# End of the attention stage: filler products, last sums in two PSUM banks, one copy on another engine, transposes last

## The chip, the cores and the metric

One core of a Trainium2 chip runs the whole kernel. The metric is the time of one execution on the device in microseconds (us). PE is TensorE, DVE is VectorE, ACT is ScalarE, POOL is GpSimd, SP is SyncE, whose queue issues the DMAs. Where the text writes L625, it means line 625 of the kernel before.

## What is computed

Attention with rotary positions over 4 batches of 8 heads, 576 positions, head width 64, all in float32; then a soft mixture of 8 experts with 4 slots each; then a two-layer network. The part that matters here is the middle one. `logits` are the products of the 2304 tokens x (width 512) with `phi` for 32 slots; a softmax over the tokens gives the weights with which the tokens are summed into slot inputs; these go through the first and second layer of their expert.

```python
logits = x @ phi
d = logits - logits.max(0, keepdims=True)
d = np.exp(d)
d /= d.sum(0, keepdims=True) + 1e-09
slot_input = d.T @ x
...
    h = np.maximum(slot_input[e] @ w1[e], 0.0)
    slot_out[e] = h @ w2[e]
```

A softmax over the slots of each token, from the same logits, later combines the outputs of the slots.

## The kernel before, in words

The heads are worked in 16 pairs, four pairs to a batch of 576 tokens. The first three batches of tokens have their logits, exponentials and sums made while the attention of later pairs runs (`batch`). The last batch cannot hide behind attention, so it is split in two halves of its tokens, `half(0)` with 256 and `half(1)` with 320 of them, that overlap with each other. Everything here is issued in an order written out by hand: each engine runs its own instructions strictly in the order in which the program lists them, and semaphores make an engine wait for what another one writes. The program lists the steps of the two halves as calls `h0[k]()` and `h1[k]()` (L945 to L970), where k counts the functions that `half` returns:

- 0 `logits` (L546): products of the tokens with phi, on PE. 1 `logits2`.
- 2 `soft` (L568): the maximum over the tokens (L569) and a few steps on one column, on DVE.
- 3 `expo` (L577): the exponential with its sum on ACT (L578), and scale factors; a scaling of the sums so far on DVE (L581) or the scaled small identity `ss` (L585).
- 4 `keep` (L587): ACT copies the logits to SBUF, for the later combine step.
- 5 `d_t` (L590): PE transposes the exponentials, 32 slots x 128 tokens at a time, into PSUM, and DVE copies them to `d` in SBUF (L600).
- 6 `s_mm` (L602): the sums, products of `d` with the tokens; L609 and, for the 64 tokens left over in half 1, L614. In half 1 the sums of the first two column blocks are in rows 0 to 63 and those of the last two in rows 64 to 127 of one PSUM bank.
- 8 `merge` (L616): DVE scales half 0's sums and adds them to the sums so far, `s_b[0]`.
- 7 `slots` (L619): ACT copies the two parts of half 1's sums to SBUF in two steps (L623); PE transposes and adds the merged sums (four products with `ss`, L625) and half 1's sums (four products, L629) in one PSUM tile; DVE copies the result to `si` (L630). What is passed as `between` is issued between the two groups of products.
- 9 `total` (L632): the sum of the weights, on DVE.

After half 1's `d_t`, five PE transposes of the kept logits (`lt3`, L964) go as `between` into `slots`, and ACT copies them to `lt` (L968, L969). Then the first layer begins (`layer1`, L990): 64 f32 products with 32 weight columns and 512 moving columns. It needs `si` and the weights `w`, whose loads SP issues (`load_w`, L129), the later ones when earlier tiles release their places in SBUF. A product of f32 operands runs as two instructions on PE, an f32 transpose as one. PSUM tiles come from pools of fixed banks: `ps_m` and `ps_u` have one bank each, `ps_mx` one pair of banks, `ps_st` two pairs.

Of the kernel before, what the change touches and what calls it, by code (L numbers as in the profile page):

```python
# [7 lines left out]
F32 = mybir.dt.float32  # L8
# [3 lines left out]
ACTF = mybir.ActivationFunctionType  # L12
# [9 lines left out]
NSLOT = 32  # L22
# [43 lines left out]
def attn_softmoe_mlp_kernel(ctx: ExitStack, tc: tile.TileContext, qk, v, cst, phi, w1, w2, w_in, w_out, out):  # L66
    nc = tc.nc
    pe, act, dve, pool, sp = nc.tensor, nc.scalar, nc.vector, nc.gpsimd, nc.sync
# [13 lines left out]
    cst_sb = const.tile([128, 256], F32, tag="cst", name="cst_sb")  # L82
    ident = cst_sb[:, 0:128]
# [106 lines left out]
    with tc.manual_schedule():  # L190
        with ExitStack() as t1:
            def mkpool(name, bufs, space=None):
                return t1.enter_context(tc.tile_pool(name=name, bufs=bufs, **({"space": space} if space else {"side": left})))
# [8 lines left out]
            ps_mx = mkpool("ps_mx", 1, PSUM)  # L202
            ps_u = mkpool("ps_u", 1, PSUM)
            ps_m = mkpool("ps_m", 1, PSUM)
# [177 lines left out]
            et, er, u_ps, xt, xq = {}, {}, {}, {}, {}  # L382
# [63 lines left out]
            def x_c(p, c):  # L446
                return xq[p][:, 2 * c:2 * c + 2].rearrange("p h d -> p (h d)")
# [90 lines left out]
            hb = []  # L538

            def half(h):  # L540
                i, o, w_ = 3 + 2 * h, QO[h], QN[h]
                xs = [xt[12 + j] for j in range(4)]
                d = p_r.tile([128, 3, NSLOT], F32, tag=f"dh{h}", name=f"dh{h}")
                ps = {}
# [44 lines left out]

                def d_t():  # L590
                    if h:
                        t = ps_mx.tile([128, 2, 512], F32, tag="mx", name=f"dps{i}")[:, 0]
                    else:
                        t = ps_u.tile([128, 512], F32, tag="u", name=f"dps{i}")
                    for c in range(2):
                        pe.transpose(t[:, NSLOT * c:NSLOT * c + NSLOT], ps["dt"][0:32, 128 * c:128 * c + 128], ident[0:32, 0:32])
                    for r in HEAD[0:2 * h]:
                        pe.matmul(t[r, 2 * NSLOT:3 * NSLOT], lhsT=ps["dt"][0:32, 256:320], rhs=ident[0:32, 0:32], start=True, stop=True, skip_group_check=True)
                    n = 2 + h
                    dve.tensor_copy(out=d[:, 0:n], in_=t[:, 0:NSLOT * n].rearrange("p (c s) -> p c s", c=n))  # L600

                def s_mm():  # L602
                    t = ps["s"] = (ps_m if h else ps_u).tile([128, DM], F32, tag="m" if h else "u", name=f"sps{i}")
                    js = (0, 2, 1, 3) if h else range(4)
                    for j in js:
                        w = slice(128 * j, 128 * j + 128)
                        g = 64 * h * (j // 2)
                        for c in range(2):
                            pe.matmul(t[g + 32 * c:g + 32 * c + 32, w], lhsT=d[:, c], rhs=x_c(12 + j, 2 * h + c), start=j % (2 if h else 4) == 0, stop=h == 0, skip_group_check=True)  # L609
                    for j in js:  # L610
                        for hd, r in enumerate(HEAD[0:2 * h]):
                            o = 128 * j + 64 * hd
                            g = 64 * (j // 2) + 32 * hd
                            pe.matmul(t[g:g + 32, o:o + 64], lhsT=d[r, 2], rhs=xq[12 + j][r, 8], start=False, stop=True, skip_group_check=True)  # L614

                def merge():  # L616
                    dve.scalar_tensor_tensor(out=s_b[0][0:64], in0=ps["s"][0:64], scalar=sc[0:64, 3:4], in1=s_b[0][0:64], op0=ALU.mult, op1=ALU.add)
# [1 line left out]
                def slots(between):  # L619
                    o = hb[1][:, 0:DM]  # L620
                    t = ps_st.tile([128, 2, 512], F32, tag="st", name="slots")[:, :, 0:2 * NSLOT].rearrange("p b (k s) -> p b k s", k=2)
                    for r, c in ((slice(0, 64), slice(0, 256)), (slice(64, 128), slice(256, 512))):
                        act.activation(out=o[r, c], in_=ps["s"][r, c], func=ACTF.Copy)  # L623
                    for k in range(4):
                        pe.matmul(t[:, k // 2, k % 2], lhsT=s_b[0][:, 128 * k:128 * k + 128], rhs=ps["ss"], start=k % 2 == 0, stop=False, skip_group_check=True)  # L625
                    between()
                    for k in range(4):
                        r = HEAD[k // 2]
                        pe.matmul(t[:, k // 2, k % 2], lhsT=o[r, 128 * k:128 * k + 128], rhs=stack_i[r, 0:NSLOT], start=False, stop=True, skip_group_check=True)  # L629
                    dve.tensor_copy(out=si.rearrange("p (b k) s -> p b k s", b=2), in_=t)  # L630

                def total():  # L632
# [4 lines left out]
                    dve.reciprocal(out=den, in_=den)  # L637

                return logits, logits2, soft, expo, keep, d_t, s_mm, slots, merge, total

            CHUNKS = [[(128 * c, min(128, S - 128 * c)) for c in range(5)]] * 4
# [227 lines left out]
            a, b = rot[0], rot[1] = rotary(0), rotary(1)  # L869
# [65 lines left out]
            t = ps_mx.tile([128, 2, 512], F32, tag="mx", name="u_31")  # L935
# [9 lines left out]
            h0, h1 = hb[0], hb[3]  # L945
# [3 lines left out]
            assert not tasks, tasks  # L949
            h0[3]()  # L950
            h1[0]((3,))
            h0[5]()
            h1[2]()
            h0[4]()
            h1[3]()
            h0[6]()
            h1[5]()
            h0[8]()
            h1[4]()
            t = ps_mx.tile([128, 2, 512], F32, tag="mx", name="lt3_ps")  # L960

            def lt3():
                for i, (o, n) in enumerate(CHUNKS[3]):
                    pe.transpose(t[0:n, 0, NSLOT * i:NSLOT * i + NSLOT], hb[2][0:32, o:o + n], ident[0:32, 0:32])  # L964

            h1[6]()
            h1[7](lt3)
            act.activation(out=lt[:, 15:19], in_=t[:, 0, 0:4 * NSLOT].rearrange("p (c s) -> p c s", c=4), func=ACTF.Copy)  # L968
            act.activation(out=lt[0:64, 19], in_=t[0:64, 0, 4 * NSLOT:5 * NSLOT], func=ACTF.Copy)  # L969
            h1[9]()  # L970

        def pool2(name, bufs, space=None, st=ctx, **kw):
# [300 lines left out]
    t = ps_o.tile([128, 512], F32, tag="o", name="g0_ps")[:, 0:128]  # L1273
# [28 lines left out]
    for n, (j, k) in enumerate(seq):  # L1302
        ghi, glo = gt.pop((j, k))
        for i in range(NI):
            if (j, k, i) not in ((0, 0, 0), (0, 0, 1), (0, 0, 2)):
                products(j, k, i, ghi, glo)
            t = ops[j, i]
# [7 lines left out]
            if k == 15:  # L1315
                o = g2.tile([128, DM], F32, tag="os", bufs=6, name=f"os{j}_{i}")
# [52 lines left out]
```

## Time and profile before

| | |
|---|---|
| median of 3 runs | 563.58 us (562.36 to 564.84) |
| profiled execution, whole | 562.48 us |
| span of its instructions | 560.7 us |
| PE busy in the span | 542.5 us, 97% |
| DVE, ACT, POOL busy | 312.7, 298.8, 112.5 us |
| mean granted clock of PE | 0.993 of full speed |

The profile is of one execution, and the sums that are made from its rows stand against its own 562.48 us. The span runs from the first instruction to the last; 1.8 us of the whole lie around it. Times in the rows are us from the start of the span. A matmul's end is modelled, and its products overlap, so the time from the start of one group to the start of the next tells more than their busy time.

### The profile page before, as it was taken

The numbers are of one execution on the slowest core, as the hardware profiler recorded it, in microseconds if no ns is written. First come the engines' busy times: TensorE is split into PE (matmuls) and PEld (weight loads), VectorE is DVE, ScalarE is ACT, GpSimd is POOL, SyncE is SP. The second block draws the span as 40 slices with busy tenths as digits, with TensorE's granted clock in tenths as the row PEclk, the third lists the DMA queues.
The fourth block names the chain that finished last, engine by engine and source line by source line (L and its number), as shares of the span: only waits on it lengthen the run. The fifth ranks groups of instructions, "written<-read, shape, count | busy, mean of one in ns | idle before, by whom it ended". The sixth has DMA issues, their size and how long they took to land.

```text
span 560.7 us, 15277 instructions
## 1 busy us (share of the span) xinstructions
PE 542.5 (97%) x6283; PEld 437.4 (78%) x6283; DVE 312.7 (56%) x826; ACT 298.8 (53%) x582; POOL 112.5 (20%) x105
## 2 busy tenths in 40 slices
PE   8989999999999999999999989999999999999996
PEld 5668888888888988888862347788888888888885
DVE  4667666676665567654130448877454444644442
ACT  3656666666676566664420346775443444533342
POOL 3475433312333323200000031412000000000000
PEclk9999999999999999999998999999999999999999
DMA  8325777645664675663799885461030000300002
GB/s 330 117 88 196 237 235 264 211 159 173 225 219 147 211 275 180 224 213 92 297 344 365 290 351 191 131 198 63 2 112 1 1 0 0 114 1 1 0 1 112
DMA packets 38720, 89.31 MB, mean 159 GB/s; under 512 B 10598, under 2 KB 13948, under 8 KB 36732
## 3 DMA queue, kind: packets, MB, share of 16 engines
q1 hardware_dynamic: 38652, 88.36, 45.3%
q8 instruction: 49, 0.80, 0.6%
q14 instruction: 19, 0.16, 0.1%
HBM read 78.20 MB, written 7.60 MB: 153 GB/s over the span
## 4 chain that ended last, share of the span: by engine, by line
PE 81%; ACT 7%; DVE 5%; issue 3%; DMA 2%; SPq 1%; ACTq 0%; DVEq 0%
PE ops L1266 11%; PE ops L1268 11%; PE ops L1267 11%; PE u L431 10%; PE st L398 7%; PE psmx L327 3%; PE l L996 3%; PE hps L1173 3%; ACT e L402 3%; PE st_r L411 3%; PE l L1017 3%; PE xps L459 2%; ACT relu L335 2%; PE u L425 2%; PE psmx L343 2%
## 5 line engine op out<-in xcount | busy, mean ns | idle before, releaser
L1180 DVE TENSOR_TENSOR hps<-hps,g 128x384 f32<-128x384 f32 x96 | 50.5, 562 | 81.5 <-ACT g L1177 81.4
L1177 ACT ACTIVATE g<-hps 128x384 f32<-128x384 f32 x96 | 43.2, 489 | 85.0 <-PE hps L1173 84.7
L348 DVE CUSTOM_DVE_ANT_0 relu<-psmx,relu 128x288 f32<-128x288 f32 x142 | 59.4, 454 | 44.7 <-ACT e L402 38.3
L402 ACT ACTIVATE e<-st 128x512 f32<-128x512 f32 (+1 forms) x128 | 76.4, 650 | 10.4 <-PE st L398 10.4
L431 PE MATMUL u<-v,e 128*64 128x65 f32 x2048 | 80.1, 224 | 0.3 <-ACT e L402 0.3
L1266 PE MATMUL ops<-wo_hi,ghi 128*128 128x512 f32 x198 | 77.8, 393 | 0.7 <-ACT ghi L1183 0.7
L1267 PE MATMUL ops<-wo_lo,ghi 128*128 128x512 f32 x198 | 77.4, 391 | 0.3 <-POOL wo_lo L1161 0.3
L1268 PE MATMUL ops<-wo_hi,glo 128*128 128x512 f32 x198 | 77.6, 392 | 0.0
L431 PEld LDWEIGHTS u<-v,e 128*64 128x64 f32 x2048 | 70.9, 137 | 6.7 <-issue 2.6
L335 ACT ACTIVATE relu<-psmx 128x576 f32<-128x576 f32 x63 | 40.9, 651 | 52.5 <-PE psmx L327 40.6
L277 POOL TENSOR_TENSOR raw<-raw,tab 128x576 f32<-128x576 f32 x28 | 40.3, 1439 | 114.4 <-DMA raw<-in_qk_dram 68.3
L1186 DVE TENSOR_TENSOR glo<-hps,ghi 128x384 fp32r<-128x384 f32 x96 | 50.0, 552 | 4.0
L1183 ACT ACTIVATE ghi<-hps 128x384 fp32r<-128x384 f32 x96 | 46.2, 491 | 10.4 <-DVE hps L1180 10.3
L1268 PEld LDWEIGHTS ops<-wo_hi,glo 128*128 128x128 f32 x198 | 37.2, 188 | 8.1 <-DVE glo L1186 0.3
L1266 PEld LDWEIGHTS ops<-wo_hi,ghi 128*128 128x128 f32 x198 | 37.2, 188 | 7.9 <-ACT ghi L1183 0.9
L1267 PEld LDWEIGHTS ops<-wo_lo,ghi 128*128 128x128 f32 x198 | 37.2, 188 | 7.1 <-POOL wo_lo L1161 0.8
L274 POOL TENSOR_TENSOR raw<-raw,tab 128x576 f32<-128x576 f32 x28 | 41.3, 1475 | 0.0
L398 PE MATMUL st<-hi 64*128 64x256 f32 (+1 forms) x256 | 39.3, 301 | 0.0
L398 PE MATMUL st<-hi,lo 64*128 64x256 f32 (+1 forms) x256 | 38.2, 292 | 0.0
L398 PE MATMUL st<-mq,neg_a 64*128 64x256 f32 (+1 forms) x256 | 38.2, 292 | 0.0
L398 PE MATMUL st<-lo,hi 64*128 64x256 f32 (+1 forms) x256 | 38.2, 292 | 0.0
L1266 PE MATMUL ops<-wo_hl,ghi 128*128 128x512 f32 x90 | 35.2, 391 | 0.0
(228 smaller groups left out, 993.5 us busy)
## 6 DMA issues: line engine op xcount, KB each, us to landing
w<-in_w_dram SPq DMA_DIRECT2D x64, 512.0 KB
raw<-in_qk_dram SPq DMA_DIRECT2D x14, 1152.0 KB
w_out_raw<-in_w_out_dram SPq DMA_DIRECT2D x16, 512.0 KB
w_in_raw<-in_w_in_dram SPq DMA_DIRECT2D x12, 512.0 KB
v<-in_v_dram SPq DMA_DIRECT2D x16, 325.0 KB
out_dram<-os SPq DMA_DIRECT2D x18, 256.0 KB
w_in<-w_in SPq DMA_DIRECT2D x8, 256.0 KB
w_in_raw<-in_w_in_dram SPq DMA_DIRECT2D x2, 1024.0 KB
```

The lines of the kernel that those rows point to most:

```text
L335: act.activation(out=r, in_=pair[:, :, 0:HS], func=ACTF.Relu)
L348: dve.tensor_tensor_reduce(out=r[:, hd], in0=t[hd], in1=r[:, hd], scale=1.0, scalar=-3.0e38, op0=ALU.add, op1=ALU.max, accum_out=mxs[p % 2 ...
L398: pe.matmul(st[:, hd, 0:n], lhsT=a, rhs=b, start=i == 0, stop=i == 3, skip_group_check=True)
L402: act.activation(out=e[:, :, 0:n], in_=st[:, :, 0:n], func=ACTF.Exp, scale=0.125)
L431: pe.matmul(u[q:q + 64, 2 * i + hd], lhsT=e[:, hd, o:o + 64], rhs=x[:, hd], start=n == 0 and i + hd == 0, stop=n == 4, skip_group_check=True)
L1177: act.activation(out=g[i], in_=t[i], func=ACTF.Sigmoid)
L1180: dve.tensor_tensor(out=t[i], in0=t[i], in1=g[i], op=ALU.mult)
L1183: act.activation(out=ghi[:, i], in_=t[i], func=ACTF.Copy)
L1186: dve.tensor_tensor(out=glo[:, i], in0=t[i], in1=ghi[:, i].bitcast(F32), op=ALU.subtract)
L1266: pe.matmul(t, lhsT=a, rhs=wo_hi[k], start=k == 0, stop=False)
L1267: pe.matmul(t, lhsT=a, rhs=wo_lo[k], start=False, stop=False)
L1268: pe.matmul(t, lhsT=b, rhs=wo_hi[k], start=False, stop=k == 15)
```

## The change

`half(0)`'s copy of its transposed exponentials moves from DVE to ACT, and its `keep` is listed ahead of it. Half 1's sums go to two PSUM banks, one for rows 0 to 63 and one for rows 64 to 127, and their two copies to SBUF are made by ACT and by DVE. Products of the identity with 64 constant columns, whose results nobody reads, are listed on PE at five places: 3 after half 0's transposes, 3 after its sums, 4 after half 1's transposes, 3 inside `slots` in the place of the logit transposes, 4 after these, which now come behind `slots`. Nothing else is added, and no DMA is touched.

```diff
--- before.py
+++ after.py
@@ -589,7 +589,8 @@
 
                 def d_t():
                     if h:
-                        t = ps_mx.tile([128, 2, 512], F32, tag="mx", name=f"dps{i}")[:, 0]
+                        ps["two"] = ps_mx.tile([128, 2, 512], F32, tag="mx", name=f"dps{i}")
+                        t = ps["two"][:, 0]
                     else:
                         t = ps_u.tile([128, 512], F32, tag="u", name=f"dps{i}")
                     for c in range(2):
@@ -597,21 +598,27 @@
                     for r in HEAD[0:2 * h]:
                         pe.matmul(t[r, 2 * NSLOT:3 * NSLOT], lhsT=ps["dt"][0:32, 256:320], rhs=ident[0:32, 0:32], start=True, stop=True, skip_group_check=True)
                     n = 2 + h
-                    dve.tensor_copy(out=d[:, 0:n], in_=t[:, 0:NSLOT * n].rearrange("p (c s) -> p c s", c=n))
+                    o, i_ = d[:, 0:n], t[:, 0:NSLOT * n].rearrange("p (c s) -> p c s", c=n)
+                    if h:
+                        dve.tensor_copy(out=o, in_=i_)
+                    else:
+                        act.activation(out=o, in_=i_, func=ACTF.Copy)
 
                 def s_mm():
                     t = ps["s"] = (ps_m if h else ps_u).tile([128, DM], F32, tag="m" if h else "u", name=f"sps{i}")
+                    ts = ps["ss2"] = (t, ps["two"][:, 1] if h else t)
                     js = (0, 2, 1, 3) if h else range(4)
                     for j in js:
                         w = slice(128 * j, 128 * j + 128)
                         g = 64 * h * (j // 2)
+                        t = ts[j // 2]
                         for c in range(2):
                             pe.matmul(t[g + 32 * c:g + 32 * c + 32, w], lhsT=d[:, c], rhs=x_c(12 + j, 2 * h + c), start=j % (2 if h else 4) == 0, stop=h == 0, skip_group_check=True)
                     for j in js:
                         for hd, r in enumerate(HEAD[0:2 * h]):
                             o = 128 * j + 64 * hd
                             g = 64 * (j // 2) + 32 * hd
-                            pe.matmul(t[g:g + 32, o:o + 64], lhsT=d[r, 2], rhs=xq[12 + j][r, 8], start=False, stop=True, skip_group_check=True)
+                            pe.matmul(ts[j // 2][g:g + 32, o:o + 64], lhsT=d[r, 2], rhs=xq[12 + j][r, 8], start=False, stop=True, skip_group_check=True)
 
                 def merge():
                     dve.scalar_tensor_tensor(out=s_b[0][0:64], in0=ps["s"][0:64], scalar=sc[0:64, 3:4], in1=s_b[0][0:64], op0=ALU.mult, op1=ALU.add)
@@ -619,8 +626,9 @@
                 def slots(between):
                     o = hb[1][:, 0:DM]
                     t = ps_st.tile([128, 2, 512], F32, tag="st", name="slots")[:, :, 0:2 * NSLOT].rearrange("p b (k s) -> p b k s", k=2)
-                    for r, c in ((slice(0, 64), slice(0, 256)), (slice(64, 128), slice(256, 512))):
-                        act.activation(out=o[r, c], in_=ps["s"][r, c], func=ACTF.Copy)
+                    a, b_ = ps["ss2"]
+                    act.activation(out=o[0:64, 0:256], in_=a[0:64, 0:256], func=ACTF.Copy)
+                    dve.tensor_copy(out=o[64:128, 256:512], in_=b_[64:128, 256:512])
                     for k in range(4):
                         pe.matmul(t[:, k // 2, k % 2], lhsT=s_b[0][:, 128 * k:128 * k + 128], rhs=ps["ss"], start=k % 2 == 0, stop=False, skip_group_check=True)
                     between()
@@ -949,24 +957,32 @@
             assert not tasks, tasks
             h0[3]()
             h1[0]((3,))
+            h0[4]()
             h0[5]()
             h1[2]()
-            h0[4]()
+            busy = ps_m.tile([128, 512], F32, tag="m", name="busy0")
+
+            def fill_up(n, t):
+                for _ in range(n):
+                    pe.matmul(t[:, 0:64], lhsT=ident, rhs=cst_sb[:, 0:64], start=True, stop=True, skip_group_check=True)
+
             h1[3]()
+            fill_up(3, busy)
             h0[6]()
+            fill_up(3, busy)
             h1[5]()
             h0[8]()
             h1[4]()
+            fill_up(4, busy)
+            h1[6]()
+            busy = ps_u.tile([128, 512], F32, tag="u", name="busy1")
+            h1[7](lambda: fill_up(3, busy))
             t = ps_mx.tile([128, 2, 512], F32, tag="mx", name="lt3_ps")
-
-            def lt3():
-                for i, (o, n) in enumerate(CHUNKS[3]):
-                    pe.transpose(t[0:n, 0, NSLOT * i:NSLOT * i + NSLOT], hb[2][0:32, o:o + n], ident[0:32, 0:32])
-
-            h1[6]()
-            h1[7](lt3)
+            for i, (o, n) in enumerate(CHUNKS[3]):
+                pe.transpose(t[0:n, 0, NSLOT * i:NSLOT * i + NSLOT], hb[2][0:32, o:o + n], ident[0:32, 0:32])
             act.activation(out=lt[:, 15:19], in_=t[:, 0, 0:4 * NSLOT].rearrange("p (c s) -> p c s", c=4), func=ACTF.Copy)
             act.activation(out=lt[0:64, 19], in_=t[0:64, 0, 4 * NSLOT:5 * NSLOT], func=ACTF.Copy)
+            fill_up(4, busy)
             h1[9]()
 
         def pool2(name, bufs, space=None, st=ctx, **kw):
```

## Rows read from the trace of the kernel before

**Rows 1.** The page: span, busy time and instructions of each engine, PE's clock in 40 slices.

```profile
span 560.7 us, 15277 instructions
...
PE 542.5 (97%) x6283; PEld 437.4 (78%) x6283; DVE 312.7 (56%) x826; ACT 298.8 (53%) x582; POOL 112.5 (20%) x105
...
PEclk9999999999999999999998999999999999999999
```

**Rows 2.** Busy time by stretch: us, each engine's busy us, granted clock, DMA share, GB/s.

```profile
288.00:290.00 2.00, 1.61 (x22) 1.19 (x22) 0.89 (x4) 1.12 (x4) 0.00 (x0) 1.00 0.96 332
290.00:292.00 2.00, 1.66 (x39) 1.37 (x39) 0.91 (x2) 0.50 (x2) 0.00 (x0) 1.00 1.04 394
292.00:294.00 2.00, 1.61 (x21) 1.40 (x24) 0.36 (x3) 0.61 (x3) 0.00 (x0) 0.73 1.02 390
294.00:296.00 2.00, 2.00 (x12) 0.54 (x16) 0.69 (x4) 0.00 (x0) 0.00 (x0) 0.50 1.04 384
298.00:300.00 2.00, 2.00 (x16) 0.51 (x12) 0.00 (x0) 0.00 (x0) 0.00 (x0) 0.56 0.91 305
330.00:332.00 2.00, 1.66 (x19) 1.29 (x22) 1.82 (x5) 2.00 (x5) 1.20 (x1) 1.00 1.04 418
332.00:334.00 2.00, 1.28 (x34) 0.93 (x26) 0.33 (x2) 0.56 (x2) 2.00 (x3) 1.00 1.04 432
```

**Rows 3.** The chain of waits in order of time: start us, us, engine and line.

```profile
287.81 0.23 DVE dh L600
288.04 0.41 DVE mb L569
...
293.60 0.30 DVE si L630
```

**Rows 4.** The timeline, 284 to 300: start us, us, engine, line, instructions, idle before and releaser.

```profile
285.01 0.66 PE L459 MATMUL xps<-cst_sb,x 128*64 128x128 f32 x8
...
285.50 0.28 PE L461 MATMUL xps<-cst_sb,x 128*64 128x64 f32 x4
...
285.71 1.82 PE L559 MATMUL lgh<-xt,phi_sb 128*32 128x320 f32 x24
...
286.94 0.49 DVE L581 TENSOR_SCALAR s_b<-s_b,sc 128x512 f32<-128x512 f32 x1 [1.43 <-ACT sc L580]
...
287.46 0.31 PE L596 MATMUL dps<-cst_sb,last_logits 32*128 32x32 f32 x2
...
288.09 1.07 PE L609 MATMUL sps<-x,dh 128*32 128x128 f32 x16 [0.32 <-DVE dh L600]
...
289.45 0.30 PE L596 MATMUL dps<-cst_sb,last_logits 32*128 32x32 f32 x2 [0.29 <-ACT last_logits L578]
...
290.21 0.73 DVE L617 SCALAR_TENSOR_TENSOR s_b<-sps,sc,s_b 64x512 f32<-64x512 f32 x1
...
290.35 0.65 PE L609 MATMUL sps<-x,dh 128*32 128x128 f32 x16 [0.36 <-DVE dh L600]
...
291.28 1.08 PE L625 MATMUL slots<-ss,s_b 128*128 128x32 f32 x8
291.47 0.78 ACT L623 ACTIVATE last_logits<-sps 64x256 f32<-64x256 f32 x2 [1.57 <-PE sps L614]
...
292.29 0.46 PE L964 MATMUL lt_ps<-cst_sb,last_logits 32*128 32x32 f32 x5
...
292.68 0.88 PE L629 MATMUL slots<-cst_sb,last_logits 64*128 64x32 f32 x8
292.78 0.28 ACT L968 ACTIVATE lt<-lt_ps 128x128 f32<-128x128 f32 x1 [0.53 <-PE lt_ps L964]
...
293.95 6.50 PE L996 MATMUL l<-w,si 128*32 128x512 f32 x32 [0.39 <-DVE si L630]
```

**Rows 5.** The timeline, 328 to 336: the first group of transposes.

```profile
329.40 0.86 PE L1079 MATMUL cst<-cst_sb,ch 128*128 128x128 f32 x5
```

**Rows 6.** Waits of SP's DMA queue, 250 to 360: us in all, times, longest.

```profile
SPq L129 <- PE l L996: 15.5, 4, 8.2
```

## The prediction

> **What bounds the kernel now.** I read the page first: TensorE (PE) is busy for 542.5 of the 560.7 us, and its clock row has one dent, a single digit, just behind the middle of the span [rows 1]. The busy times by stretch give the dent its size [rows 2]: the granted clock is 1.00 up to 292, 0.73 in 292:294, 0.50 in 294:296, 0.56 in 298:300, and full again later. [...] So the clock is low from 292.92 to 299.76. What the engine did before the fall stands in the rows before it: 288 to 294 have 1.6 us of 2 busy each, with waits in between and small products. Being busy by these rows does not hold the clock by itself: 332:334 shows less, 1.28 us of 2, and the clock stays at 1.00.
>
> What runs at half speed is mostly the first layer: it starts at 293.95 [rows 4] and fills its stretches [rows 2]. 299.76 - 293.95 = 5.81 us at half clock is 2.90 us of work, so 2.90 us is what a full clock gives back here.
>
> The chain of waits shows what stands in front of it [rows 3]: the copy of the first half's weights on VectorE (DVE), the maximum of the second half on the same engine behind that copy, then, after ACT's (ScalarE's) exponential and the products, the last copy. The timeline has PE's own order [rows 4]. From start to start: transposes 287.46, first sums 288.09, transposes 289.45, last sums 290.35, slot products (L625) 291.28, five logit transposes 292.29, second slot products (L629) 292.68, first layer 293.95.
>
> **The change part by part, in the order of time.** The price of a filler: it is a product of 128 weight columns with 64 moving columns in f32, which runs as two instructions. The nearest row is L625, 128x128 weights with 32 columns: its eight instructions start at 291.28 and the next group starts at 292.29, 1.01 us with the hand-over, 0.126 each [rows 4]. So four fillers cost 1.01 us, three 0.76, all seventeen 34 x 0.126 = 4.28 us. That width doubles costs nothing extra if the weight load sets the pace, as the same row suggests. Lower end: x products with half as many weight columns, eight from 285.01 to 285.50, 0.061 each [rows 4]; I take the nearer row. Upper end: a single instruction's 0.135 (1.08 / 8).
>
> *Copy to ACT, keep first.* DVE loses the copy of 0.23 us; the maximum, which started at 288.04 behind it on the chain [rows 3], can start when the logits end, 285.71 + 1.82 = 287.53 (DVE's scaling is done at 287.43 [rows 4]). With the start-up of a DVE step I take 287.65, so the maximum and the exponential come 0.39 us earlier, and the second transposes could start at 289.45 - 0.39 = 289.06. On ACT the copy is priced by a 128x128 copy, 0.28 us [rows 4], against 0.23, so the weights are no more than 0.05 us later; below nothing there is no reason for. It fits on ACT between keep and the exponential at 288.4. Keep already came before in time, so its move costs nothing.
>
> *Three fillers before the first sums.* Two transposes take 0.16 (five took 0.39), to 287.62; fillers to 288.38. The first sums start there in place of 288.09: +0.29.
>
> *Three fillers after them.* The sixteen instructions need about 0.91 us (I take 1.07 less 0.16 for the last one's tail), to 289.29; fillers to 290.05. The second transposes were at 289.45 and could have come at 289.06: what DVE gained is covered by fillers, and PE stands +0.60.
>
> *Four fillers after the second transposes.* These take about 0.38 to issue (an estimate: 0.16 as above, and four narrower products in 0.22), 290.43; fillers to 291.44, where the last sums start: before, 290.35, +1.09. Their weights are ready at 290.05 + 0.90 = 290.95 (0.90 is 289.45 to 290.35), so 0.49 of this is over the wait. The merge on DVE (0.73 us [rows 4]) also comes later, by 0.6, and ends near 291.6, still ahead of the slot products at 292.37.
>
> *Two banks, two engines.* ACT's two half copies took 0.78 us in series [rows 4]; now one half each runs on ACT and DVE at once, about 0.4 us. The copies end near 292.9; PE is in the slot products until 293.38 and then in fillers, so this is worth nothing here. Without fillers it would be covered too.
>
> *Transposes last, fillers in their place.* Three fillers replace five transposes: 0.76 against 0.39, +0.37; L629 starts at 294.14 against 292.68, +1.46. L629 took 0.88 us, part of it at the low clock; I take 0.5 to issue at full clock (ends: 0.4 and 0.88). Then transposes 0.39 and four fillers 1.01: the first layer can start at 296.04 on PE. The si copy is ready long before: L629 ends by 295.0, copy 0.30 [rows 3], 295.4 with hand-overs. ACT's two logit copies move behind too; nobody waits for them before the combine step, behind the first layer. Start +2.09.
>
> *Loads.* No DMA is added. The weight loads at this point wait for PE's first layer to release slots [rows 6], so they follow it in both directions.
>
> *Sum.* +2.09 for the later start, -2.90 for the full clock: -0.81 us. The profiled execution took 562.48; 561.7. That execution is 1.1 us below the median 563.58, and the runs shown spread from 562.36 to 564.84, so against the median this is -0.33%.
>
> [...] From 329.40 on PE transposes in groups of four and five, with copies between (the first such group: [rows 5]), and 330:332 and 332:334 have a clock of 1.00 [rows 2]: no transpose there pulled it down. [...]
>
> **The rivals.**
>
> *The clock falls all the same* (0.27), the one on the slower side. Place: between the last sums and the first layer. The fillers resemble L625, wide weight loads and few columns, and L625 is just what ran when the clock fell, with PE busy. The fillers' columns are twice as many, and they replace real waits, which speaks against it. Price: a low stretch as long as the one seen, 6.84 us, now filled without waits, costs 3.42 us: 561.7 + 3.4 = 565.1, 2.6 us above the profiled execution. It decides as soon as a low stretch lasts longer than 1.6 us within the first layer, since 0.81 us is all that the forecast gains. A low stretch half as long again would cost 1.7 us more (566.8).
>
> *The fillers fit into the waits* (0.15). At the lower end, 0.061 per instruction, three take 0.37 and four 0.49; following the same steps the first sums start at 288.09, the second transposes at 289.37, the last sums at 290.27, L629 at 292.58, the first layer at 293.96, no later than before. Then the full 2.90 us stays: 559.6. For it: PE's waits in 288 to 294 are 1.1 us of 6 by busy time, more by start times. Against: L625 itself, whose load width is the fillers' own. [...] The row shows 126 ns with hand-over and decides.
>
> *A later stage takes the gain back* (0.08): the first layer ends 0.8 us earlier but weights or narrow steps behind it keep their times: 562.5. Against it: these loads are released by that very layer [rows 6].
>
> **How the numbers follow.** The forecast itself has 0.50. Its own range is 561.3 to 562.4: the later start from 1.7 (fillers at 0.115, the eight of L625 without tail and hand-over) to 2.8 (fillers at 0.135 and L629 at its full 0.88). Over all, 8 in 10 lie in 560.0 to 565.2: below it most of the second rival, above it the longer low stretch. About 0.5% is what a measurement of this kernel can tell from no change, 2.8 us: under 560.8 is faster, over 566.4 slower. Faster 0.20: the second rival and a little of the forecast's lower end, as other executions may lose more to the clock than the profiled one. Slower 0.08: the part of the first rival with a longer low stretch. Same 0.72.
>
> **What would show it.** Right: granted clock 1.00 from 280 to 310; the first layer at 295.5 to 296.5, at full pace from its start; second maximum near 287.65; second transposes held by PE's fillers and not by ACT; the half copies on ACT and DVE side by side. Wrong: a 0.5 in the clock between 290 and 303; the first layer starting before 295, which makes the fillers cheaper than L625; or a first layer that ends 0.8 us earlier while the end of the span does not move.

## The result, and the profile after

The changed kernel takes 564.74 us (median of 20 runs, 562.74 to 566.87), the kernel before, run beside it, 561.68 us (20 runs, 558.53 to 564.84). The ratio is 1.0057, 95% interval 1.0039 to 1.0075: slower by 3.1 us, between 2.2 and 4.2. The forecast was 561.7 us, 0.8 below the profiled execution of the kernel before, no change that can be told. The profiled execution took 566.87 us, the longest of the twenty, so its parts are read one by one and the sum is made with all runs. Rows of the changed kernel and of the experiments carry the line numbers of their own kernels; a filler is a row that writes the tile `busy`.

The page of the changed kernel, the lines that answer to [rows 1]: 34 more instructions on PE (the 17 fillers), 4.4 us more span, and the dent is still there.

```profile
span 565.1 us, 15346 instructions
...
PE 546.9 (97%) x6317; PEld 442.2 (78%) x6317; DVE 312.7 (55%) x826; ACT 298.8 (53%) x582; POOL 112.8 (20%) x105
...
PEclk9999999999999999999998999999999999999999
```

Busy time by stretch of the changed kernel, in the columns of [rows 2]:

```profile
292.00:294.00 2.00, 1.94 (x42) 1.51 (x41) 0.72 (x2) 0.38 (x1) 0.00 (x0) 1.00 1.03 392
294.00:296.00 2.00, 2.00 (x23) 1.88 (x22) 0.23 (x2) 0.00 (x0) 0.00 (x0) 1.00 0.96 346
296.00:298.00 2.00, 2.00 (x19) 1.25 (x20) 0.82 (x6) 0.35 (x2) 0.00 (x0) 0.76 0.97 345
298.00:300.00 2.00, 2.00 (x16) 0.51 (x12) 0.00 (x0) 0.00 (x0) 0.00 (x0) 0.50 0.68 262
...
338.00:340.00 2.00, 2.00 (x9) 1.61 (x8) 0.77 (x2) 0.18 (x1) 0.00 (x0) 0.50 0.01 4
```

The fillers did fill: from 288 to 296 PE is busy 1.94 us or more in every 2 us, where [rows 2] had 1.61 to 1.66 up to 294. The clock fell all the same, in 296:298, and stayed at 0.5 through 298:300, which is the sign that the prediction named for being wrong; in this execution it fell once more at 338. So in this execution a PE that showed no wait (2.00 of 2 us busy from 294 on) did not keep its clock (0.76, then 0.50).

The chain of the changed kernel, start us, us, engine, tile and line:

```profile
288.00 0.24 PE dps L597 x2
288.24 0.81 PE busy L967 x6
289.06 1.00 PE sps L616 x16
290.05 0.81 PE busy L967 x6
290.87 0.24 PE dps L597 x2
291.10 0.23 PE dps L599 x4
291.34 1.05 PE busy L967 x8
292.39 0.04 issue
...
293.43 1.01 PE slots L633 x8
294.44 0.70 PE busy L967 x6
295.14 0.57 PE slots L637 x8
295.71 0.39 PE lt_ps L982 x5
296.10 1.03 PE busy L967 x8
297.13 12.10 PE l L1012 x96
```

Of [rows 3] nothing is left: VectorE's copies are off the chain, and all of it is PE. The fillers have 0.81 + 0.81 + 1.05 + 0.70 + 1.03 = 4.40 us of it.

The waits of PE between 286 and 298 in the kernel before say how much room there was (engine, what waited, for what: us in all, times, longest); the changed kernel has no row there at all:

```profile
PE sps L609 <- DVE dh L600: 0.7, 2, 0.4
PE l L996 <- DVE si L630: 0.4, 1, 0.4
PE dps L596 <- ACT last_logits L578: 0.3, 1, 0.3
```

1.4 us of waits were filled with 4.4 us of products. Counted from the start of the first half's transposes (287.46 before, 287.94 after; that offset was there before the change begins, and from execution to execution it varies more: 286.63 and 288.98 in two of the changed kernel), PE's steps in the timelines:

| step starts, us after the first transposes | before | forecast | after | without fillers (e1) |
|---|---|---|---|---|
| first sums | 0.62 | 0.92 | 1.05 | 0.62 |
| second transposes | 1.98 | 2.59 | 2.86 | 1.62 |
| last sums | 2.88 | 3.98 | 4.49 | 2.52 |
| second slot products | 5.21 | 6.68 | 7.13 | 4.46 |
| first layer | 6.48 | 8.58 | 9.13 | 5.51 |

What was foreseen off PE's path is there. In the timeline of the changed kernel (columns as in [rows 4]):

```profile
288.07 0.49 DVE L569 TENSOR_REDUCE mb<-lgh 128x1 f32<-128x320 f32 x1 [0.17 <-PE lgh L559]
...
288.28 0.22 ACT L605 ACTIVATE dh<-dps 128x64 f32<-128x64 f32 x1 [0.63 <-PE dps L597]
...
292.43 0.11 PEld L616 LDWEIGHTS sps<-x,dh 128*32 128x32 f32 x2 [0.20 <-PE busy L967]
...
293.52 0.38 ACT L630 ACTIVATE last_logits<-sps 64x256 f32<-64x256 f32 x1 [3.55 <-PE dps L621]
293.52 0.43 DVE L631 COPY last_logits<-dps 64x256 f32<-64x256 f32 x1 [1.23 <-PE dps L621]
```

The maximum starts 0.13 us after the transposes, where it stood at 0.49 by the timeline of before; the two half copies run side by side. The third row was not foreseen: the last sums wait 0.20 us for the fillers, with which they share the pool of PSUM banks (busy0 and the second half's sums both come from ps_m).

**The end of the span.** Before, the last copy starts at 556.52 and the span ends at 560.7, 4.2 us later. After, it starts at 560.12 and the span ends at 565.1, 5.0 us later. The last row of each chain, of before and then of after:

```profile
556.52 0.69 DVE os L1318
```

```profile
560.12 0.69 DVE os L1334
```

The transfers of the changed kernel in 560:565 (queue, kind: packets, MB, share of 16 engines):

```profile
q1 hardware_dynamic: 514, 0.92, 49.8%
q14 instruction: 1, 0.01, 0.4%
```

Besides the outputs there is one packet of instructions (8 KB, on queue q14). In the trace of before the same stretch (553 to 561) has no q14 row. In all profiles taken, the time from the last product's end to the span's end is 4.21 or 4.22 us in the three of the kernel before and 4.97 or 4.98 in the three of the kernel after.

### The profile page after: what moved, and what is told of

Same layout as the page of the kernel before. It is cut to its first block, busy times and chain, and to the rows that moved or that the text cites. A ratio compares the mean times of both kernels' runs of the same rounds, so it can differ in the third digit from the quotient of the medians.

```text
span 565.1 us, 15346 instructions
## 1 busy us (share of the span) xinstructions
PE 546.9 (97%) x6317; PEld 442.2 (78%) x6317; DVE 312.7 (55%) x826; ACT 298.8 (53%) x582; POOL 112.8 (20%) x105
## 4 chain that ended last, share of the span: by engine, by line
PE 79%; ACT 7%; DVE 6%; issue 5%; DMA 1%; POOL 1%; SPq 0%; ACTq 0%; DVEq 0%; POOLq 0%
PE u L431 10%; PE ops L1283 10%; PE ops L1282 10%; PE ops L1284 10%; PE st L398 7%; PE psmx L327 3%; PE l L1012 3%; ACT e L402 3%; PE st_r L411 3%; PE l L1033 3%; PE hps L1189 3%; PE xps L459 2%; ACT relu L335 2%; PE u L425 2%; PE psmx L343 2%
```

## The experiments

**Theory.** The fillers are longer than the waits they cover, and narrow products do not hold the clock; so the start of the first layer is lost and little comes back. **Rivals:** the fillers do hold the clock and something else costs the time (the banks, the copies, the order); or the clock falls in some executions and not in others whatever stands there, and two profiles are no measure of it.

Timed kernels are given with their ratio to the kernel before. "Full clock" counts runs whose mean granted clock is 0.998 or more; one low stretch of 3.41 us, the shorter of the two lengths that the profiles have, alone takes 1.7 us, 0.003 of 562, so these runs had none of that length. "Lost" is the mean over all runs of (1 - clock) x 562 us. It holds a part that costs nothing, the drop behind the last product: 0.8 us in the profile of before, 0.9 in that of after, 1.3 in e5's, none in r1's. The kernel before, in three lots of runs, was at full clock in 12 of 76 and lost 2.8, 3.5 and 3.4 us; the kernel after in 4 of 20, and lost 2.3.

**e1: the change without its fillers** (five calls of fill_up left out; copy on ACT, two banks and the transposes last stay)

```diff
-            fill_up(3, busy)
...
-            h1[7](lambda: fill_up(3, busy))
+            h1[7](lambda: None)
```

> The changed kernel without its 17 filler products; the copy on ACT, the two banks and the transposes last stay. Theory A (the fillers' PE time over the waits is the loss, 2.6 us of later start of the first layer in the changed kernel's trace, and the clock gives too little of it back): from the first half's transposes to the first layer, 6.49 us before and 9.12 us changed, it now takes 5.2 to 5.7 us; the clock falls to 0.5 for 6.8 us as before; time 0.5 to 1.5 us under the kernel before, 3.5 to 4.5 us under the changed one. Rival B (the other edits cost: the copy on ACT, the half copy on DVE, the transposes on the path): that stretch stays over 7 us and the time is 1 us or more over the kernel before.

560.86 us (558.87 to 562.30, 12 runs; before 561.66), ratio 0.9990 (0.9968 to 1.0012). Full clock in 3 of 12, lost 1.7. The timeline of e1 shows what bounds PE without fillers:

```profile
288.86 1.07 PE L616 MATMUL sps<-x,dh 128*32 128x128 f32 x16 [0.31 <-ACT dh L605]
...
290.76 0.30 PE L616 MATMUL sps<-x,dh 128*32 128x128 f32 x2 [0.36 <-DVE dh L603]
...
293.74 1.74 PE L1001 MATMUL l<-w,si 128*32 128x512 f32 x8
```

Two waits are left, 0.31 and 0.36 us. The transposes in last place cover the one before the first layer (0.39 before), and the copy on ACT has removed the one before the second transposes (0.29 before). The first layer starts at 5.51, 3.62 us earlier than with fillers. And the clock is not worse for their absence (1.7 lost, against 2.3). The fall in e1's profile lasts 3.41 us, not the 6.8 that were expected, and the gain over the kernel before is not clear of noise.

**e2: the kernel before, with the 17 fillers and nothing else**

```diff
+            fill_up(3, busy)
             h0[6]()
+            fill_up(3, busy)
...
```

> The kernel before with the 17 filler products at the same places and nothing else of the change. Theory A: the stretch from the first half's transposes to the first layer is 9.2 to 9.8 us, time 2.5 to 4 us over the kernel before, like the changed kernel or a little above. Rival B: the stretch is under 8 us and the time within 1 us of the kernel before.

565.55 us (563.81 to 569.30, 7 runs), ratio 1.0092 (1.0058 to 1.0127), full clock in 1 of 7, lost 3.5. The timeline of e2 (PE alone, 287 to 298) has the first layer at 9.25:

```profile
287.42 0.31 PE L596 MATMUL dps<-cst_sb,last_logits 32*128 32x32 f32 x2
...
296.67 1.92 PE L1008 MATMUL l<-w,si 128*32 128x512 f32 x15
```

The fillers alone are enough for a loss of this size. That the maximum is later again moves nothing here: the second transposes stand at 2.86 as in the changed kernel, since PE is in its fillers.

**e3: fillers 1, 0, 2, 0, 1 in place of 3, 3, 4, 3, 4**

```diff
-            fill_up(3, busy)
+            fill_up(1, busy)
             h0[6]()
-            fill_up(3, busy)
...
```

> The changed kernel with 4 fillers in place of 17, where its waits are (1, 0, 2, 0, 1 in the five places). Theory A: the stretch from the first half's transposes to the first layer is 5.3 to 6 us, the clock falls nearly as in the kernel before, time 0.5 to 1.5 us under the kernel before. Rival C (any product in the waits is enough to hold the clock): clock 1.00 to the end of the first layer in the profile and in most runs, time 3 to 4 us under the kernel before.

561.35 us (559.33 to 564.52, 12 runs), ratio 0.9998 (0.9976 to 1.0020), full clock in 5 of 12, first layer at 6.08. The gain of 0.5 to 1.5 us that was expected did not come. What fits costs little (0.57 us of start against e1) and, as narrow products, brings nothing that can be measured.

**e4: as many fillers of another shape.** In each of the five places two groups of four products that stand side by side in the array (32 weight columns each) with 256 moving columns, in place of three or four of 128 weight columns with 64.

```diff
-                for _ in range(n):
-                    pe.matmul(t[:, 0:64], lhsT=ident, rhs=cst_sb[:, 0:64], ...)
+                for _ in range(2):
+                    for r in range(0, 128, 32):
+                        pe.matmul(t[r:r + 32, 0:256], lhsT=ident[:, 0:32], rhs=cst_sb, ...)
```

> The changed kernel with each place's fillers replaced by two groups of four products that have 32 weight columns and 256 moving columns each, four of them side by side in the array: about 0.86 us a place, 4.3 us in all against 4.6 us measured for the 17 narrow ones. Theory A with the addition that the narrow products are why the clock still falls: the clock stays at 1.00 from 280 to 310 in the profile and mean clock is 0.998 or more in most runs, stretch from the transposes to the first layer 8.6 to 9.2 us, time 1 to 2 us under the changed kernel and 0 to 2 us over the kernel before. Rival D (the width of the fillers does not matter, the clock falls anyway): falls as in the changed kernel, time within 0.7 us of it.

563.38 us (562.12 to 565.42, 12 runs), ratio 1.0036 (1.0018 to 1.0055). Full clock in 9 of 12, lost 1.2. The first layer starts at 9.39 (8.6 to 9.2 expected), later than in the changed kernel, and the time is still lower. The 0.86 us a place is an estimate that the first layer's rows bear out: at full clock four of its instructions with 512 columns take 0.43 us (after, 300.48 to 302.20), so the sixteen of a place, with 256, 0.86. In e4's chain a place takes 0.96 to 1.04. PE's rows of the two kernels, same stretches (us, PE busy, granted clock, DMA share, GB/s); e10, further down, has the changed kernel's own fillers and a profile in which only one low stretch falls:

e4:

```profile
294.00:296.00 2.00, 2.00 (x26) 1.00 1.05 393
296.00:298.00 2.00, 2.00 (x33) 1.00 1.03 357
```

e10:

```profile
294.00:296.00 2.00, 2.00 (x22) 0.90 1.08 353
296.00:298.00 2.00, 2.00 (x12) 0.50 1.01 363
```

Both show PE busy for all of each stretch; one keeps the clock, the other doesn't. In these runs the shape of the fillers decided how often it was kept, their presence did not: the 17 narrow ones had a full clock in 4 of 20 runs (after), 1 of 7 (e2) and 2 of 12 (e10), the wide ones in 9 of 12, and e1 without any in 3 of 12. And the kernel that mostly keeps it is still slower than the one before: 0.76 us of that is the end of the span, and its fillers cost more than the clock gives back (1.2 lost, against 2.8).

**e5: wide products only where PE waits** (a group of 192 columns and one of 256, over the two waits of e1; no other fillers)

```diff
+            wide(192, busy)
             h0[6]()
             h1[5]()
             h0[8]()
             h1[4]()
+            wide(256, busy)
             h1[6]()
```

> The kernel without fillers, with two groups of four wide products (32 weight columns, 192 and 256 moving columns, four side by side), one in PE's wait for the first half's weights and one in the wait for the second half's: 0.32 and 0.43 us. Theory A (the fall of the clock is worth 2.4 us in the median of the kernel before, fillers lose because they stand over the waits): stretch from the transposes to the first layer 5.5 to 6.1 us, mean clock 0.998 or more in most runs (before: 8 of 30), time 1.5 to 2.5 us under the kernel before and lower than both kernels. Rival E (two short groups are not enough): clock 0.996 or less in more than half of the runs, time as without fillers, within 1 us of the kernel before.

560.17 us (558.48 to 563.30, 12 runs; before 562.23), ratio 0.9976 (0.9957 to 0.9994), full clock in 8 of 12. The chain of e5:

```profile
286.43 0.24 PE dps L597 x2
286.67 0.46 PE busy L967 x8
287.13 0.92 PE sps L616 x16
...
288.52 0.61 PE busy L967 x8
289.13 0.04 issue
...
292.16 7.91 PE l L1009 x69
```

(The expectation has 8 of 30 runs of the kernel before at full clock; the record has 7.) First sums at 0.62, as in e1: the first group, 0.46 us (0.32 expected), is free. The last sums are 0.30 later (2.82 against 2.52), since the second group, 0.61 us (0.43 expected), is longer than its wait of 0.36. The first layer is at 5.80. Against e1, which has no fillers, no gain is shown: 0.29 us of later start stands against 0.3 less lost (1.4 and 1.7), and the intervals of the two ratios overlap.

**e6: e5 with a third group of 256 columns between the slot products**

```diff
-            h1[7](lambda: None)
+            busy = ps_u.tile([128, 512], F32, tag="u", name="busy1")
+            h1[7](lambda: wide(256, busy))
```

> As the kernel with wide products in two waits, and a third group of 256 moving columns between the two groups of slot products, where PE has little wait. Theory A: stretch longer by 0.4 to 0.6 us than with two groups, time 0.3 to 0.6 us above it if its clock holds as often; lower than it only if the third group is what holds the clock (rival E).

560.42 us (559.38 to 561.65, 12 runs), ratio 0.9975 (0.9958 to 0.9992), full clock in 11 of 12, lost 0.7. The third group puts the first layer 0.57 us later (6.37), and the time is that of e5; 11 of 12 against 8 of 12 are too few runs to say that the third group makes the clock surer.

**e7: e1 with one bank and both half copies on ACT**

```diff
-                    ts = ps["ss2"] = (t, ps["two"][:, 1] if h else t)
+                    ts = ps["ss2"] = (t, t)
...
-                    dve.tensor_copy(out=o[64:128, 256:512], in_=b_[64:128, 256:512])
+                    act.activation(out=o[64:128, 256:512], in_=b_[64:128, 256:512], func=ACTF.Copy)
```

> The kernel without fillers, with half 1's sums back in one bank and both half copies on ACT in series. Theory A (two banks and two engines are worth nothing while PE is in the slot products): stretch 5.5 to 5.65 us, as without fillers (5.51). Rival F (the series of copies is on the path once the transposes are not between): stretch 5.8 us or more.

559.01 us in one run. The second slot products start at 4.46 after the transposes, as in e1: two banks with two engines buy nothing on the path. The end of the span, however, is 4.01 us after the last product, against 4.96 in e1.

**e8: e1 with the first half's copy back on VectorE** (and keep back behind it)

```diff
-                    if h:
-                        dve.tensor_copy(out=o, in_=i_)
-                    else:
-                        act.activation(out=o, in_=i_, func=ACTF.Copy)
+                    dve.tensor_copy(out=o, in_=i_)
...
-            h0[4]()
             h0[5]()
             h1[2]()
+            h0[4]()
```

> The kernel without fillers, with the first half's copy back on DVE and keep listed where it was. Theory A (this copy is what shortens the chain by the 0.36 us that the second transposes came earlier): second transposes 1.95 to 2.0 us after the first ones in place of 1.62, stretch 5.8 to 5.95 us. Rival: stretch stays at 5.5.

560.27 us in one run. The second transposes go back from 1.62 to 1.98, just where they were before. So the copy on ACT is worth 0.36 us to a kernel without fillers. Its first layer is at 5.99 (5.8 to 5.95 expected; its clock is low from 292.23). Its end of span is 4.67.

**r1 and r2, r3 and r4: both kernels again, one profile each, unchanged.** They ask whether one profile's dent may be taken for the kernel's.

> A second look at the changed kernel, unchanged, for where its clock falls. Theory A (the fall moves against the program from execution to execution, and the narrow fillers leave the stretch ahead of the first layer near enough to it): a low stretch of 3.4 or 6.8 us that begins between 289 and 298, or none; stretch from the transposes to the first layer 9.0 to 9.8 us by where it begins. Rival G (what the changed kernel loses to the clock is mainly the fall at the start of the last stage, seen at 338): no low stretch before 300, one at 330 to 342.

> A third look at the changed kernel, the same expectations as for the second look.

> A second look at the kernel before, unchanged. Theory A: the low stretch begins elsewhere than at 292.93 (anywhere from 289 to 296) or is missing; its stretch from the transposes to the first layer is 6.1 to 6.8 us, and a run without the fall takes 558.5 to 560. Rival: the fall stands at the same place of the program as in the first look.

> A third look at the kernel before, the same expectations as for the second look.

The changed kernel: no fall in r1 (564.54 us), one from 295.29 of 3.41 us in r2 (564.21 us). The kernel before: from 291.98 for 6.83 us in r3 (562.01 us), from 293.09 for 3.41 us in r4 (560.88 us), where the profile of the forecast had 6.84. The first layer of r1, with no fall ahead of it, starts at 9.13 like the one that the forecast is judged by: the start is the fillers' doing, not the clock's. And a fall is not all that sets one execution's time: r1, without one, took longer than r2, because its first transposes stand at 288.98 and r2's at 286.63, ahead of everything that the change touches. PE's rows of r1:

```profile
296.00:298.00 2.00, 2.00 (x23) 1.00 1.02 289
298.00:300.00 2.00, 2.00 (x22) 1.00 1.02 376
```

and of r4, the kernel before with the shorter dent:

```profile
292.00:294.00 2.00, 1.61 (x21) 0.77 1.05 402
294.00:296.00 2.00, 2.00 (x12) 0.50 1.05 389
```

**e9: e5 with e7's edit** (wide groups in the two waits, one bank, both half copies on ACT)

> The kernel with wide products in two waits (32 weight columns, 192 and 256 moving), with half 1's sums back in one bank and both half copies on ACT. Theory H (0.76 us of the end of the span come from one 8 KB fetch of instructions that falls among the last output packets, and which copy is on which engine decides whether it does): no instruction packet in the last 5 us, last PE product to end of span 4.0 to 4.3 us in place of 4.97, stretch from the transposes to the first layer 5.8 to 5.95 us, time 0.5 to 1.2 us under the kernel with two banks, so 2.5 to 3.3 us under the kernel before. Rival I (the tail follows something else): tail 4.97 us, time as with two banks.

558.46 us (557.82 to 561.38, 12 runs; before 562.07), ratio 0.9957 (0.9933 to 0.9980): the fastest of all, 0.43% below the kernel before; with the ratios of both to that kernel, 0.9957 / 1.0057, 1.0% below the changed one. First layer at 5.80 as in e5; the end of the span 4.02 after the last product, against 4.97 in e5. Full clock in 8 of 12. What its wide groups add is not shown: the same kernel without them, e7, took 559.01 us in its one run, with a fall. The profile of e9 is one of the other four, with no fall ahead of the first layer, but one in 332:334, long after it; the changed kernel's own profile has such a late one too, at 338.

```profile
332.00:334.00 2.00, 1.27 (x32) 0.87 0.09 37
334.00:336.00 2.00, 2.00 (x9) 0.50 0.00 0
```

**e10: the changed kernel, all its fillers, with e7's edit**

> The changed kernel with half 1's sums back in one bank and both half copies on ACT, all 17 fillers as they are. Theory H: stretch 9.1 to 9.6 us as in the changed kernel, no instruction packet in the last 5 us, tail 4.0 to 4.3 us, time 0.5 to 1.2 us under the changed kernel, so 1.8 to 2.6 us over the kernel before: that much is left of the loss when the tail is as before. Rival I: tail 4.97 us and 2.8 to 3.4 us over the kernel before.

563.68 us (561.06 to 565.68, 12 runs; before 562.07), ratio 1.0030 (1.0010 to 1.0051), first layer at 9.63 (the fall, at 295.59, catches the last fillers here: 1.53 us in place of 1.03). Full clock in 2 of 12, lost 2.2; e9, run beside it with wide groups, has 8 of 12. It is 1.6 us over the kernel before, where 1.8 to 2.6 were expected. The span (561.8 us) ends 4.01 us after the last product, 0.96 less than in the changed kernel. The last row of its chain:

```profile
557.79 0.69 DVE os L1334
```

The transfers of e10 in 556:562, its last 5.8 us, have no q14 row:

```profile
## 3 DMA queue, kind: packets, MB, share of 16 engines
q1 hardware_dynamic: 837, 1.52, 68.1%
```

So the longer end has nothing to do with the fillers: it is there with them (after, e4) and without (e1, 4.96), and it goes with that one edit (e7, e9, e10). What the edit moves is the place of the instruction packets on q14. In the trace of the changed kernel one comes 2.55 us after the last product, and a share of the last output lands 3.90 us after that product; without such a packet the last share lands at 2.85. The half copy is not alone in moving it: e8 leaves that copy on VectorE and takes the first half's copy back there, and its packet comes 0.58 us after the last product. By the count of VectorE's instructions in the traces the packet comes at 4.5 to 4.8 us, behind the end of the span, with 1088 (e7, e9, e10) or 1089 (before, e2), at 2.55 with 1090 (after, e1, e4, e5) and at 0.58 with 1091 (e8). That the packet holds up the share is argued from its place among the outputs; that both come and go together was seen in each of these profiles; that the count is the cause was not tested.

## Why the prediction was wrong

At full clock the changed kernel has a median of 563.17 us (4 runs), the kernel before 559.33 (7 of the 30 run beside e1): 3.8 us more. Two terms make up most of that. The fillers put the first layer at 9.13 where a kernel before with a full clock would have it at about 6.3, an estimate (its second slot products at 5.21, 0.70 from their start to the copy's in the changed kernel, 0.35 from the copy's start to the first layer before): 2.9. The end of the span has 0.76. Together 3.6. What the clock gives back is the difference of what the runs lost, 3.2 (mean of the three lots) less 2.3: 0.9, give or take 0.7 by the spread of the runs; the three lots are other ones than the 20 runs of the result, whose clocks of the kernel before are not on record. 2.9 + 0.76 - 0.9 = 2.8 us, beside the 3.1 measured. The same sum for e2 is 3.0 for the start, nothing for the end (4.22), 0.7 more lost than by the kernel before: 3.7, beside 3.9.

**The step that failed: "2.90 us is what a full clock gives back here", and with it that the fillers give a full clock.** It failed twice. The fillers did not hold the clock: full in 4 of 20 runs, hardly more often than in the kernel before (12 of 76) and no more than in e1 without them (3 of 12). And the 2.90 was read from one execution with a long dent (6.84 us: at 0.50, the clock of 294:296, the 0.73 and 0.56 of [rows 2] are 1.08 and 1.76 us of 2 that are low); r4 has half of it, and some executions of the kernel before have none. With the fillers' narrow shape, some 0.9 of 2.90 came back. The doubt was in the first rival, which is the one that happened: the clock falls all the same, with PE busy, at the end of the place named (297.06, where the first layer starts; 295.29 in r2), and the fillers resemble L625. That its price, 565.1, is 0.4 from the median is luck: a low stretch was mostly 3.41 us and not 6.84 (granted clock 0.996 or 0.997 in 11 of 20 runs), and the two terms below were missing.

**The start, mis-sized: +2.09 forecast, +2.65 measured**, +2.9 against a full clock. The price of an instruction was right: 4.40 / 34 = 0.129 us with 64 moving columns against 0.126 with the 32 of L625. What was too low stands between the fillers: two transposes take 0.24 and not 0.16, the first sums 1.00 and not 0.91, six transposes 0.47 and not 0.38. Each had its last product's tail or a narrower width taken off, and the chain shows that PE's next group starts no earlier. These are 0.26; the two groups of six fillers have 0.05 more each, the eight 0.08 with their hand-over, and some 0.07 is left, which may be what the wait at the shared bank adds to the path (no run gives these fillers another bank). Together 0.51: the last sums stand at +1.61 in place of +1.09, and that is nearly all of the 0.56.

**Not in the sum: the end of the span, +0.76.** It was taken as unchanged without a row. No wait of the change leads there.

**Right:** the maximum 0.36 and the exponential 0.41 earlier with the copy on ACT (0.39 forecast), covered by fillers (e2, e8); two banks worth nothing on the path (e7); the half copies side by side; the second transposes held by fillers and not by ACT; no DMA on the path ahead of the first layer. The rival that the fillers fit is out by the chain (0.129 each, not 0.061); that a later stage takes the gain back is out too, as it asks for a first layer that ends earlier, and r1 starts it 2.65 later even at a full clock.

**The transposes** in last place did no harm to the clock in these runs: e4, e5, e6 and e9 all keep them behind the slot products and are at full clock in 36 of 48. Nor do they set how often it holds: the changed kernel, at full clock in 4 of 20, has the same five behind the slot products.

Still open is what in the shape of a product counts for the clock. e4 changed three things at once, the number of weight columns, of moving columns, and of products that stand side by side; they were not tried apart.

## What to carry to other kernels

Before you fill an engine's waits, add them up (1.4 us here) and price what you put in: here 4.4 us of fillers over those waits put the first layer 2.65 us later, and of the 2.90 us of one long dent some 0.9 came back. Take what a dent costs from many executions' granted clocks, not from one profile. Where filler work is to hold TensorE's clock, try wide products first, a group or two about as long as the wait (here full clock in 8 of 12 runs each, e5 and e9), and not many narrow ones (7 of 39: after, e2, e10). And time the kernel without any filler beside it: here leaving them out (e1) was not shown to be slower than the best of them with the same copies (e5).

## What was not expected of the hardware

The place and length of the fall differ from execution to execution of one kernel: before, from 292.93 for 6.83, from 291.98 for 6.83, from 293.09 for 3.41 us; after, from 297.06, from 295.29, or not at all. That is a part of the spread of the kernel before, 558.4 to 564.8 us. Against the program it moves too: it came 4.90, 5.47 and 5.63 us after the first transposes in the three profiles of the kernel before. What moves it was not shown.

In these profiles PE's busy share did not tell whether the clock holds. It fell after 8 us with PE busy 1.94 of 2 us or more (288 to 296 of after), in narrow products, and held through 332:334 of before at 1.28 of 2 [rows 2].

Which engine does a small copy near the middle moved the end of the span by 0.76 to 0.96 us, together with the place of an 8 KB packet of instructions among the last outputs. In these profiles a longer end came with each one that fell among the last outputs (4.67 to 4.98 us against 4.01 to 4.22), and one share of these landed late (3.90 against 2.85 us after the last product).
